# Seeding a PSUM bank, staging high parts in PSUM, longer runs for down weights and earlier raw loads in an attention, expert and feed-forward kernel

## The chip, the cores and the metric

The kernel runs on one core of a Trainium2 chip: TensorE multiplies matrices into PSUM, VectorE, ScalarE and GpSimd work elementwise, SyncE (SP) issues the transfers. GpSimd works on SBUF alone; VectorE and ScalarE read and write PSUM too. The metric is the device time of one execution in microseconds. Three runs took 2031.32 to 2033.63 us, median 2032.89.

## The reference

```python
scores = q @ k.T / sqrt(64)                       # 4 batches, 8 heads, 576 positions
mask: heads 0-3: 0 <= i - j < 32;  heads 4-7: i >= j and i % 32 == j % 32
x = (softmax(where(mask, scores, -1e9)) @ v)      # to 2304 tokens x 512
P = exp(x @ w_gate - max)                         # 2304 x 8
8 times: P /= P.sum(1) + 1e-9; P /= P.sum(0) + 1e-9; P *= 2304 / 8
x = sum over e of P[:, e] * (relu(x @ w1[e]) @ w2[e])         # 8 experts, 512 -> 1024 -> 512
h = x @ w_in                                                  # 512 -> 2048
out = (h * sigmoid(1.702 * h)) @ w_out                        # 2048 -> 512
```

All in float32. The kernel keeps that precision by splitting each operand into a high part (rounded to TensorE's fp32r) and a low part (the rest), and adds three products: high by high, high by low, low by high.

## The kernel before, in words

**Units.** The 2304 tokens are three blocks of 768. A unit is 256 hidden columns of one block: 32 units (8 experts by 4) for each block, then 8 for each block of the feed-forward layer, 120 in all. The first expert phase (block 0) is units 0 to 31, the second stage (blocks 1 and 2, where `seven(i)` holds) units 32 to 95, the ffn units 96 to 119.

**The up product** is not done as 8 block products but as 7 (`PRODUCTS`, line 44), with sums of input quarters (S1 to S4) and of weight quarters (T1 to T4). Each product is six matmuls of 384 columns (`sum_of_six`), and several add up in a PSUM bank: A takes X11, S2, S3 and X22; C takes S1 and S4; B takes X12. `product_and_after` (line 871) does what stands between the products: ScalarE copies a partial sum to SBUF (`copy_of`), VectorE adds it to a bank (`add`, line 868; line 887 for A plus a copy into B), and `activate` makes the hidden values: a high part on ScalarE (line 849), a low part on VectorE (line 852). X22 adds to bank A, so it waits until VectorE's addition of line 887 has read that bank.

**The down product** of units 0 to 31 and of the ffn is plain: six tiles a unit, six matmuls of 512 columns each (`tile_down`, lines 1080 to 1082), then VectorE adds the tile to the token sums (line 1099). In the second stage the down product is by sevens too (`chain`, line 976; VectorE adds at line 986).

**Weights.** In the first phase each unit's raw weights are loaded (`wa`, `wb`, 512 KB each), their quarters summed on GpSimd, and split by `split_into` (line 235): ScalarE rounds the high part (line 244), GpSimd or VectorE subtracts for the low part (line 238), a given number of pieces later, and SP stores both parts to DRAM, for the next phases (`s1moe`, `s7moe`). There VectorE makes the low parts of the up weights (w) and, for units whose first pass came too early, of recombined down weights (kw): `plan_down_sums` with `again` loads the raw down weights (raws) once more, subtracts (line 312) and splits.

**Order.** Nothing is reordered by a scheduler: the program is one list of pieces (13 a unit: 7 products and 6 down tiles), and `side[piece]` holds what is issued after that piece. Each engine takes its instructions in that order, and SP's transfers too. `piece_at(unit, k)` names a place in the list.

**PSUM** has eight banks. After the attention is done (`late`), they are A, A2, B, B2, C and three for down tiles (y, y, y3); `open_bank` alternates, and the gate's small products (`spare_bank`) borrow B or B2. While the attention still runs, A and B change places from unit to unit.

Of the kernel before, what the change touches and what calls it, by code (L numbers as in the profile page):

```python
# [47 lines left out]
    ("X12", "W21", "B", True, True),  # L48
# [8 lines left out]
def strided_attention_moe_ffn(  # L57
# [65 lines left out]
    late = []  # L123
    bank = {}
    turn_of = defaultdict(int)

    def open_bank(b, i):
# [107 lines left out]
    def split_into(t, src, kept, eng=nc.gpsimd, low=0, store=0):  # L235

        def rest():
            eng.tensor_tensor(out=t[:, 1, :], in0=src, in1=f(t[:, 0, :]), op=ALU.subtract)  # L238
# [5 lines left out]
        nc.scalar.activation(out=t[:, 0, :], in_=src, func=AF.Copy)  # L244
# [18 lines left out]
    def split_w1(i, k):  # L263
# [9 lines left out]
        if kind == "moe" and i > PLAIN:  # L273
            split_into(t, src, kept, nc.vector, *((5, 7) if PRODUCTS[k][0] == "X22" else (1, 3)))
        else:
            split_into(t, src, kept, store=2 if i > PLAIN else 0)

    def split_w2(i, ft):
        t = w2p.tile([P, 2, D], F32R, tag="w2", name="w2")
        _, kind, blk, n = UNITS[i]  # L280
        w2[i, ft] = t
        kept = sw2[n, ft].rearrange("p (h c) -> p h c", h=2) if kind == "ffn" else None
# [10 lines left out]
        split_into(t, raw[2, i][:, ft, :], kept, low=(0, 2 - ft)[i >= PLAIN], store=(0, 4)[i >= PLAIN])  # L293
# [5 lines left out]
    def plan_down_sums(dp, i, again=None):  # L299
# [14 lines left out]
        def split(k):  # L314
            t = dp.tile([P, 2, 2 * P], F32R, tag="kw", name="kw", bufs=5)
            src = down_sums[i][:, WHERE[PRODUCTS[k][1]][1], :]
            split_into(t, src, sw7[n, k].rearrange("p (h c) -> p h c", h=2), eng, 1 if again is None else 2, 3)
# [6 lines left out]
        if again is not None:  # L324

            side[piece_at(again, 0)].append(load)
# [3 lines left out]
        for m, k in enumerate(ks):  # L330
            at = piece_at(i, (6, 4)[i == S0 - 1] + m) if again is None else piece_at(again + 1, m)
# [45 lines left out]
    def plan_ahead(lo, hi):  # L377

        for n in range(AHEAD):
# [25 lines left out]
            def split_again(ft, r=r, n=n):  # L405
                t = r["kw"] if ft == 0 else r["sums"].rearrange("p q c -> p (q c)")
                t = t.rearrange("p (h c) -> p h c", h=2)
                src = r["raw"][:, ft * D : (ft + 1) * D]
                split_into(t.bitcast(F32R), src, sw2[n, ft].rearrange("p (h c) -> p h c", h=2), low=1, store=3)
# [69 lines left out]
    def input_sum(ph, m, eng):  # L479
        q = quarters(ph)  # L480
        what = PRODUCTS[m][0]
        if ph == 0:
            was = {"S3": "S1", "S4": "S2"}.get(what)
            xin[what, ph] = xin[was, ph] if was else rawp[0].tile([P, 2, NH], F32, tag=what, name=what)
        elif what == "S1":
# [5 lines left out]
            "S2": (xin.get(("S1", ph)), q["X11"], ALU.subtract),  # L491
# [921 lines left out]
```

## Time and profile before

| What | Before |
|---|---|
| median of 3 runs | 2032.89 us |
| profiled execution | 2031.87 us, span 2030.1 us, mean granted clock 0.993 |
| TensorE matmul busy | 1960.0 us (97%) |
| VectorE busy | 1610.9 us (79%) |
| GpSimd busy | 1233.5 us (61%) |
| ScalarE busy | 817.5 us (40%) |
| transfers | 548.32 MB, mean 270 GB/s |
| chain that ended last | PE 74%, DVE 13%, DMA 7%, POOL 2% |

The profile calls the engines PE (matmul), PEld (weight load), DVE (VectorE), ACT (ScalarE), POOL (GpSimd) and SP. TensorE's ends are modelled and its matmuls overlap, so its busy share is no measure of its pace; the number of matmuls in a stretch is.

How the views below are read. A row of busy time by stretch gives the stretch and its length in us, then the busy us and (x) the number of instructions of PE, PEld, DVE, ACT and POOL, then the granted clock, the mean share of the 16 DMA engines, and GB/s. A row of the waits gives the engine and line that waited, for whom, the us in total, how often, and the longest. A row of the timeline gives start, duration, engine, line, operation, and in brackets the idle time before it with what ended it. A row of the groups gives line, engine, operation, names (written <- read), shapes and count, then busy us, mean ns of one, and idle us before them with what ended it.

### The profile page before, as it was taken

How to read it: one execution, taken by the hardware profiler on the slowest of the kernel's cores; microseconds unless marked ns; L12 is line 12 of the kernel's file. 1: busy time of each engine (PE TensorE's matmuls, PEld its weight loads, DVE VectorE, ACT ScalarE, POOL GpSimd, SP SyncE). 2: the span in 40 equal slices, each digit the busy share in tenths (PEclk: the TensorE clock that was granted, in tenths of full speed). 3: DMA queues.
4: the chain of work that ended last, by engine and by line, in shares of the span. 5: the costliest groups of instructions: out<-in, count | busy, mean ns of one | idle time of the engine just before them, and what ended most of it. 6: DMA issues, size and time to landing. Idle time of an engine off the chain costs nothing.

```text
span 2030.1 us, 33823 instructions
## 1 busy us (share of the span) xinstructions
PE 1960.0 (97%) x10865; PEld 1800.8 (89%) x10865; DVE 1610.9 (79%) x2937; ACT 817.5 (40%) x2040; POOL 1233.5 (61%) x1201
## 2 busy tenths in 40 slices
PE   8999989898889999999999999999999999999999
PEld 6777778787778899999999999999999988898888
DVE  6777888897898788888788788999888666666666
ACT  6555534443445433333333433333333335533432
POOL 4443346686677777676767888878888747800200
PEclk9999999999999999999999999999999999999999
DMA  6356468999998798889888789998989957765663
GB/s 226 136 215 235 169 220 298 338 327 327 314 331 313 273 331 283 286 297 299 292 295 289 251 264 336 301 345 301 332 304 333 327 191 248 247 221 177 214 195 125
DMA packets 294640, 548.32 MB, mean 270 GB/s; under 512 B 30688, under 2 KB 75968, under 8 KB 293184
## 3 DMA queue, kind: packets, MB, share of 16 engines
q1 hardware_dynamic: 294176, 545.71, 78.3%
q8 instruction: 87, 1.43, 0.3%
q14 instruction: 89, 0.73, 0.1%
q10 hardware_dynamic: 288, 0.46, 0.1%
HBM read 384.52 MB, written 161.53 MB: 269 GB/s over the span
## 4 chain that ended last, share of the span: by engine, by line
PE 74%; DVE 13%; DMA 7%; POOL 2%; issue 2%; ACT 1%; SPq 1%; DVEq 0%; POOLq 0%; ACTq 0%
PE y L976 21%; PE pA L813 20%; PE pC L813 9%; PE y L1080 5%; PE y L1082 5%; PE y L1081 5%; PE pB L813 5%; DVE w L238 2%; DMA s1moe<-w 2%; DMA raws<-wb 2%; DMA s7moe<-kw 1%; DVE hl L852 1%; PE sc L589 1%; DVE acc L1099 1%; DVE kw L238 1%
## 5 line engine op out<-in xcount | busy, mean ns | idle before, releaser
L813 PE MATMUL pA<-xc,w 128*128 128x384 f32 x2880 | 583.1, 340 | 23.5 <-DVE pB L887 23.4
L813 PEld LDWEIGHTS pA<-xc,w 128*128 128x128 f32 x2880 | 510.5, 190 | 46.9 <-DVE pB L887 32.7
L976 PE MATMUL y<-comb,w 128*128 128x384 f32 x2688 | 538.9, 335 | 6.8 <-DVE sum L986 4.4
L976 PEld LDWEIGHTS y<-comb,w 128*128 128x128 f32 x2688 | 472.6, 188 | 9.0 <-DVE sum L986 6.1
L923 POOL TENSOR_TENSOR comb<-s,comb 128x384 fp32r<-128x384 f32 x256 | 280.9, 1109 | 71.0 <-ACT comb L918 65.7
L986 DVE TENSOR_TENSOR sum<-y,sum 128x384 f32<-128x384 f32 x420 | 230.4, 550 | 99.4 <-PE y L976 98.5
L813 PE MATMUL pC<-xc,w 128*128 128x384 f32 x1464 | 296.6, 337 | 0.0
L1080 PE MATMUL y<-w,hh 128*128 128x512 f32 x672 | 270.0, 402 | 10.2 <-ACT hh L849 9.6
L918 ACT ACTIVATE comb<-r 128x384 fp32r<-128x384 f32 x192 | 101.0, 526 | 432.1 <-DVE r L929 394.5
L1082 PE MATMUL y<-w,hl 128*128 128x512 f32 x672 | 269.7, 401 | 0.7 <-DVE hl L852 0.7
L813 PEld LDWEIGHTS pC<-xc,w 128*128 128x128 f32 x1464 | 257.9, 188 | 10.3 <-issue 0.7
L1081 PE MATMUL y<-w,hh 128*128 128x512 f32 x672 | 266.6, 397 | 0.0
L839 ACT ACTIVATE c<-pA 128x384 f32<-128x384 f32 x236 | 115.0, 487 | 145.3 <-PE pA L813 142.5
L238 POOL TENSOR_TENSOR w<-raw,w 128x512 fp32r<-128x512 f32 (+1 forms) x100 | 119.5, 1201 | 71.3 <-ACT w L244 62.7
L1080 PEld LDWEIGHTS y<-w,hh 128*128 128x128 f32 x672 | 127.6, 190 | 36.5 <-ACT hh L849 15.0
L1082 PEld LDWEIGHTS y<-w,hl 128*128 128x128 f32 x672 | 126.9, 189 | 34.0 <-DVE hl L852 5.5
L923 POOL TENSOR_TENSOR comb<-r,comb 128x384 fp32r<-128x384 f32 x64 | 68.0, 1063 | 145.1 <-ACT comb L918 144.2
L918 ACT ACTIVATE comb<-s 128x384 fp32r<-128x384 f32 x256 | 131.7, 514 | 28.8 <-POOL s L948 28.2
L813 PE MATMUL pB<-xc,w 128*128 128x384 f32 x708 | 142.7, 336 | 0.0
L1109 DVE TENSOR_TENSOR acc<-y,acc 128x512 f32<-128x512 f32 x126 | 86.5, 686 | 70.0 <-PE y L1082 69.4
L1081 PEld LDWEIGHTS y<-w,hh 128*128 128x128 f32 x672 | 127.5, 190 | 15.2
L948 POOL TENSOR_TENSOR s<-r,r 128x384 f32<-128x384 f32 x126 | 138.0, 1115 | 0.0
(154 smaller groups left out, 3015.7 us busy)
## 6 DMA issues: line engine op xcount, KB each, us to landing
w<-s1moe SPq DMA_DIRECT2D x448, 256.0 KB, 4.9
w<-s7moe SPq DMA_DIRECT2D x448, 256.0 KB, 4.9
s1moe<-w SPq DMA_DIRECT2D x216, 256.0 KB, 4.4
w<-s1ffn SPq DMA_DIRECT2D x133, 256.0 KB, 2.7
s7moe<-kw SPq DMA_DIRECT2D x128, 256.0 KB, 4.5
s7moe<-w SPq DMA_DIRECT2D x96, 256.0 KB, 4.4
w<-s2ffn SPq DMA_DIRECT2D x38, 512.0 KB, 4.0
raw<-wa SPq DMA_DIRECT2D x32, 512.0 KB, 6.7
```

Source lines behind the costliest of these rows:

```text
L238: eng.tensor_tensor(out=t[:, 1, :], in0=src, in1=f(t[:, 0, :]), op=ALU.subtract)
L813: nc.tensor.matmul(out=o, lhsT=w[:, hw, kk * P : (kk + 1) * P], rhs=x[:, hx, kk, :], start=opens and m == 0, stop=ends and m == len(todo) - 1,
L839: nc.scalar.activation(out=t, in_=bank[b][:, :NH], func=AF.Copy)
L918: nc.scalar.activation(out=t[:, 0, :], in_=part[i, q], func=AF.Copy)
L923: eng.tensor_tensor(out=t[:, 1, :], in0=part[i, q], in1=f(t[:, 0, :]), op=ALU.subtract)
L948: g.tensor_tensor(out=part[i, q], in0=part[i, a], in1=part[i, b], op=op)
L976: nc.tensor.matmul(out=o, lhsT=t[:, hw, dt * P : (dt + 1) * P], rhs=x[:, hx, :], start=(n == 0), stop=(n == 5))
L986: nc.vector.tensor_tensor(out=a, in0=o, in1=a, op=ALU.add)
L1080: nc.tensor.matmul(out=y, lhsT=hh[:, c], rhs=w[:, 0], start=(m == 0), stop=False)
L1081: nc.tensor.matmul(out=y, lhsT=hh[:, c], rhs=w[:, 1], start=False, stop=False)
L1082: nc.tensor.matmul(out=y, lhsT=hl[:, c], rhs=w[:, 0], start=False, stop=(m == 1))
L1109: nc.vector.tensor_tensor(out=a, in0=y, in1=a, op=ALU.add)
```

## The change

The copy of X11's sum goes into bank B, which X12 then adds to. The copy of A after S2 is added to C at once, and S4 adds on top. Bank B2 becomes a bank S with two halves, into which ScalarE writes the high part a second time wherever VectorE makes the low part; VectorE reads it there, and before a half is written again the subtraction that reads it is issued. Down weights lie as two column halves with their high and low parts side by side, so that a stored quarter is one run of 2 KB, and a down matmul reads its 512 columns as two runs of 256. The raw load of `again` is issued in the unit before, its splits are spread. Input sums on VectorE are done in halves, two of the four sums of unit 95 go to GpSimd, and there is one more piece between the gate's row and column steps.

```diff
-    ("X12", "W21", "B", True, True),
+    ("X12", "W21", "B", False, True),
...
         if late:
-            if b != "C" and turn_of[b] % 2:
-                pool, tag = late[0], b + "2"
-        elif i % 2:
+            if b == "A" and turn_of[b] % 2:
+                pool, tag = late[0], "A2"
+        elif i % 2 == 0:
             tag = {"A": "B", "B": "A", "C": "C"}[b]
... spare_bank
-        turn_of["B"] += 1
-        pool, tag = (late[0], "B2") if turn_of["B"] % 2 else (ps, "B")
-        return pool.tile(shape, F32, tag=tag, name=name)
+        turn_of["y"] += 1
+        if turn_of["y"] % 3 == 0:
+            return late[0].tile(shape, F32, tag="y3", name=name)
+        return ps.tile(shape, F32, tag="y", name=name, bufs=2)
... split_into
-        nc.scalar.activation(out=t[:, 0, :], in_=src, func=AF.Copy)
+        nc.scalar.activation(out=high, in_=src, func=AF.Copy)
+        if late and eng is nc.vector:
+            if not stage:
+                stage.append(late[0].tile([P, 2, 2 * P], F32R, tag="S", name="high"))
+            turn_of["S"] += 1
+            half = turn_of["S"] % 2
+            high = stage[0][:, half, :]
+            if half in staged:
+                staged[half]()
+            staged[half] = rest = once(rest)
+            nc.scalar.activation(out=high, in_=src, func=AF.Copy)
... split_w1
-            split_into(t, src, kept, nc.vector, *((5, 7) if PRODUCTS[k][0] == "X22" else (1, 3)))
+            split_into(t, src, kept, nc.vector, 1, 3)
... split_w2
-        t = w2p.tile([P, 2, D], F32R, tag="w2", name="w2")
+        t = w2p.tile([P, 2 * D], F32R, tag="w2", name="w2")
-                    c = (int(what[2]) - 1) * 2 * P
-                    kept.append((sw7[n, k].rearrange("p (h c) -> p h c", h=2), f(t)[:, :, c : c + 2 * P]))
+                    c = (int(what[2]) - 1) * D
+                    kept.append((sw7[n, k], f(t)[:, c : c + D]))
... plan_down_sums
-            side[piece_at(again, 0)].append(load)
+            side[piece_at(again - 1, 2)].append(load)
-            at = piece_at(i, (6, 4)[i == S0 - 1] + m) if again is None else piece_at(again + 1, m)
+            at = piece_at(i, (7, 4)[i == S0 - 1] + m) if again is None else piece_at(again + 1, 2 * m)
... plan_inputs
-            put(last - 1, 3, input_sum, ph, 4, v)
-            put(last - 1, 7, input_sum, ph, 5, v)
+            for h in range(2):
+                put(last - 1, 3 + h, input_sum, ph, 4, v, h)
+                put(last - 1, 6 + h, input_sum, ph, 5, v, h)
... gate_steps
-            steps += [sinkhorn_rows, lambda: None, lambda: None, sinkhorn_cols]
+            steps += [sinkhorn_rows, lambda: None, lambda: None, lambda: None, sinkhorn_cols]
... product_and_after
         if x == "X11":
-            snap["a"] = copy_of("A")
+            o = open_bank("B", i)[:, :NH]
+            nc.scalar.activation(out=o, in_=bank["A"][:, :NH], func=AF.Copy)
         elif x == "S2":
-            snap["u"] = copy_of("A")
+            add(copy_of("A"), "C", "C")
         elif x == "X12":
-            return go(i, "11", add(snap["a"], "B", "B"))
+            return go(i, "11", bank["B"][:, :NH])
         elif x == "S3":
-            if late:
-                o = open_bank("B", i)[:, :NH]
-                nc.vector.tensor_tensor(out=o, in0=bank["A"][:, :NH], in1=snap["c"], op=ALU.add)
-                return go(i, "22", o)
             return go(i, "22", add(snap["c"], "A", "B"))
         elif x == "S4":
-            return go(i, "12", add(snap["u"], "C", "C"))
+            return go(i, "12", bank["C"][:, :NH])
... down_input_sum, plan_seven
-        g = nc.vector if i == S1 - 1 else nc.gpsimd
+        eng = nc.vector if i == S1 - 1 and n % 2 else nc.gpsimd
-                put(u, 13, down_input_sum, u + 1, n)
+                put(u, 13 + (n // 2 if u + 1 == S1 - 1 else 0), down_input_sum, u + 1, n)
... tile_down
+            o = halves(y)
-            nc.tensor.matmul(out=y, lhsT=hh[:, c], rhs=w[:, 0], start=(m == 0), stop=False)
+            nc.tensor.matmul(out=o, lhsT=hh[:, c], rhs=w[:, 0], start=(m == 0), stop=False)
```

SP's queue in the first phase before, around the fifth repeated load of raw down weights (raws); kept are the 1.5 MB sums of the experts that waited for the gate:

```order
L213 DMA raw_5163<-wb 128x1024
L242 DMA s7moe<-w_5098 256x1x256 x2
L242 DMA s1moe<-w_5115 128x512
L242 DMA s7moe<-kw 128x512 x3
L1119 DMA acc<-kept 128x3072
L321 DMA raws_5207<-wb 128x1024
L206 DMA raw_5233<-wa 128x1024
```

The same place now:

```order
L214 DMA raw_5072<-wa 128x1024
L348 DMA raws_5078<-wb 128x1024
L252 DMA s1moe<-w_5039 128x512
L252 DMA s7moe<-kw 128x512
L252 DMA s1moe<-w_5055 128x512
L252 DMA s1moe<-w_5069 128x512
L252 DMA s7moe<-kw 128x512
L252 DMA s1moe<-w_5088 128x512
L252 DMA s7moe<-kw 128x512
L252 DMA s7moe<-w_5108 128x512
```

The load stands right behind the unit's first raw load, and the load of the kept sums (L1119 before, L1146 now) follows it after 16 further rows; the stores of down weights (s7moe<-w) are now 128 runs of 512 values in place of 256 of 256.

VectorE's queue in such a unit before, from X12 to the addition in front of X22:

```order
L312 TENSOR_TENSOR dsums<-raws_6417 128x256
L868 TENSOR_TENSOR pB<-pB,c 128x384
L312 TENSOR_TENSOR dsums<-raws_6417 128x256
L238 TENSOR_TENSOR w_6488<-sums,w_6488 128x256
L1099 SCALAR_TENSOR_TENSOR acc<-y,pr,acc 128x512
L852 SCALAR_TENSOR_TENSOR hl_6503<-pB,hh_6502 128x384
L312 TENSOR_TENSOR dsums<-raws_6417,dsums 128x256
L887 TENSOR_TENSOR pB<-pA,c 128x384
```

And now:

```order
L897 TENSOR_TENSOR pC<-pC,c 128x384
L248 TENSOR_TENSOR w_6546<-sums,high 128x256
L1126 SCALAR_TENSOR_TENSOR acc<-y,pr,acc 128x512
L339 TENSOR_TENSOR dsums<-raws_6329 128x256 x2
L248 TENSOR_TENSOR w_6579<-sums,high 128x256
L1126 SCALAR_TENSOR_TENSOR acc<-y,pr,acc 128x512
L881 SCALAR_TENSOR_TENSOR hl_6593<-pB,hh_6592 128x384
L339 TENSOR_TENSOR dsums<-raws_6329,dsums 128x256
L897 TENSOR_TENSOR pB<-pA,c 128x384
```

The addition to bank B after X12 is gone, the one to bank C stands ahead of X12's place, and each low part (w) reads the staged high part.

## Rows read from the trace of the kernel before

**Rows 1.** Busy time by stretch.

```profile
257.00:296.00 39.00, 35.58 (x171) 30.68 (x170) 33.71 (x79) 14.71 (x37) 16.11 (x18) 0.96 0.67 232
296.00:648.50 352.50, 317.25 (x1492) 272.30 (x1491) 317.76 (x517) 160.37 (x425) 239.74 (x253) 0.97 0.92 319
444.00:459.70 15.70, 15.70 (x80) 13.97 (x79) 15.11 (x26) 10.21 (x27) 13.24 (x15) 1.00 0.98 351
794.80:1100.60 305.80, 305.80 (x1766) 305.80 (x1766) 250.93 (x480) 99.62 (x211) 217.34 (x213) 1.00 0.87 288
1115.00:1619.00 504.00, 499.23 (x2859) 494.48 (x2858) 424.60 (x759) 176.79 (x378) 413.24 (x390) 1.00 0.89 310
1619.00:1663.70 44.70, 39.83 (x211) 38.06 (x210) 31.50 (x49) 15.64 (x29) 26.66 (x23) 0.96 0.63 205
1664.00:1800.00 136.00, 136.00 (x676) 121.17 (x675) 89.88 (x152) 66.36 (x147) 82.10 (x78) 1.00 0.69 241
1789.70:1867.90 78.20, 78.20 (x391) 70.29 (x390) 49.17 (x86) 26.58 (x55) 0.00 (x0) 1.00 0.57 186
```

**Rows 2.** Waits of TensorE from 296 to 648.5 us.

```profile
PE pA L813 <- DVE pB L887: 20.4, 15, 5.2
PE y L1080 <- ACT hh L849: 9.6, 10, 1.8
```

**Rows 3.** Timeline from 457 to 473 us: SP's queue, VectorE, TensorE.

```profile
458.15 0.59 SPq L321 DMA_DIRECT2D raws<-wb  x1
...
468.06 0.42 DVE L312 TENSOR_TENSOR dsums<-raws 128x256 f32<-128x256 f32 x1 [6.32 <-DMA raws<-wb]
...
472.31 0.69 PE L813 MATMUL pA<-xc,w 128*128 128x384 f32 x1 [5.18 <-DVE pB L887]
```

**Rows 4.** Groups of VectorE from 296 to 648.5 us.

```profile
L238 DVE TENSOR_TENSOR w<-sums,w 128x256 fp32r<-128x256 f32 x77 | 54.2, 704 | 0.0
L238 DVE TENSOR_TENSOR w<-raw,w 128x256 fp32r<-128x256 f32 x58 | 45.4, 795 | 0.0
L238 DVE TENSOR_TENSOR kw<-dsums,kw 128x256 fp32r<-128x256 f32 x36 | 36.8, 1022 | 0.0
...
L312 DVE TENSOR_TENSOR dsums<-raws 128x256 f32<-128x256 f32 x18 | 11.6, 647 | 21.8 <-DMA raws<-wb 21.8
...
L868 DVE TENSOR_TENSOR pB<-pB,c 128x384 f32<-128x384 f32 x19 | 10.5, 554 | 0.0
```

**Rows 5.** Groups of VectorE from 1900 to 2000 us, GpSimd idle.

```profile
L1109 DVE TENSOR_TENSOR acc<-y,acc 128x512 f32<-128x512 f32 x33 | 22.6, 686 | 20.0 <-PE y L1082 20.0
L862 DVE TENSOR_TENSOR hl<-sg,hh 128x384 fp32r<-128x384 f32 x26 | 14.5, 556 | 0.7
```

**Rows 6.** The same from 1664 to 1800 us, GpSimd busy.

```profile
L862 DVE TENSOR_TENSOR hl<-sg,hh 128x384 fp32r<-128x384 f32 x35 | 22.5, 643 | 0.7
```

**Rows 7.** A group of ScalarE from 296 to 648.5 us.

```profile
L244 ACT ACTIVATE w<-sums 128x256 fp32r<-128x256 f32 x77 | 31.5, 409 | 13.7 <-POOL sums L223 13.6
```

**Rows 8.** Waits of ScalarE from 296 to 648.5 us.

```profile
ACT hh L849 <- DVE pB L868: 99.9, 18, 9.3
...
ACT kw L244 <- DMA s7moe<-kw: 12.5, 11, 2.8
```

**Rows 9.** Transfers from 296 to 648.5 us; issues: count, KB each, us to landing.

```profile
DMA packets 59146, 112.38 MB, mean 319 GB/s; under 512 B 5751, under 2 KB 20439, under 8 KB 58605
...
s7moe<-w SPq DMA_DIRECT2D x57, 256.0 KB, 4.5
```

**Rows 10.** Busy time in the two stretches of 50 us with most bytes.

```profile
368.00:418.00 50.00, 47.77 (x228) 40.77 (x228) 47.06 (x71) 24.20 (x66) 35.11 (x36) 0.99 1.00 352
1438.00:1488.00 50.00, 49.24 (x283) 48.72 (x283) 41.95 (x82) 17.16 (x37) 41.20 (x39) 1.00 0.98 359
```

**Rows 11.** Waits of TensorE from 1619 to 1663.7 us.

```profile
PE y L976 <- DVE sum L986: 4.4, 2, 4.2
```

**Rows 12.** The gate's matmuls by line: ns min/median/max.

```profile
L731 PE MATMUL pl<-x,wgr x96: 326/326/350, 96.0 to 256.7; 128*32 128x192 f32 x96
```

More of the change, by code (lines that the diff above doesn't have):

```diff
@@ L123, in strided_attention_moe_ffn, with once @@
     late = []
+    stage = []
+    staged = {}
+    def once(fn):
+        todo = [fn]
+        return lambda: todo.pop()() if todo else None
     bank = {}
@@ L235, in split_into @@
     def split_into(t, src, kept, eng=nc.gpsimd, low=0, store=0):
+        high = t[:, 0]
         def rest():
-            eng.tensor_tensor(out=t[:, 1, :], in0=src, in1=f(t[:, 0, :]), op=ALU.subtract)
+            eng.tensor_tensor(out=t[:, 1], in0=src, in1=f(high), op=ALU.subtract)
         def keep():
@@ L273, in split_w1, with by_part, halves @@
         if kind == "moe" and i > PLAIN:
-            split_into(t, src, kept, nc.vector, *((5, 7) if PRODUCTS[k][0] == "X22" else (1, 3)))
+            split_into(t, src, kept, nc.vector, 1, 3)
         else:
             split_into(t, src, kept, store=2 if i > PLAIN else 0)
+    def by_part(t):
+        return t.rearrange("p (q h c) -> p h q c", q=2, h=2)
+    def halves(src):
+        return src.rearrange("p (q c) -> p q c", q=2)
     def split_w2(i, ft):
-        t = w2p.tile([P, 2, D], F32R, tag="w2", name="w2")
+        t = w2p.tile([P, 2 * D], F32R, tag="w2", name="w2")
         _, kind, blk, n = UNITS[i]
-        w2[i, ft] = t
-        kept = sw2[n, ft].rearrange("p (h c) -> p h c", h=2) if kind == "ffn" else None
+        w2[i, ft] = by_part(t)
+        kept = sw2[n, ft] if kind == "ffn" else None
         if not fresh(i):
@@ L290, in split_w2 @@
                 if what[0] == "W" and int(what[1]) == ft + 1:
-                    c = (int(what[2]) - 1) * 2 * P
-                    kept.append((sw7[n, k].rearrange("p (h c) -> p h c", h=2), f(t)[:, :, c : c + 2 * P]))
-        split_into(t, raw[2, i][:, ft, :], kept, low=(0, 2 - ft)[i >= PLAIN], store=(0, 4)[i >= PLAIN])
+                    c = (int(what[2]) - 1) * D
+                    kept.append((sw7[n, k], f(t)[:, c : c + D]))
+        split_into(by_part(t), halves(raw[2, i][:, ft, :]), kept, low=(0, 2 - ft)[i >= PLAIN], store=(0, 4)[i >= PLAIN])
     down_sums = {}
@@ L406, in split_again @@
                 t = r["kw"] if ft == 0 else r["sums"].rearrange("p q c -> p (q c)")
-                t = t.rearrange("p (h c) -> p h c", h=2)
                 src = r["raw"][:, ft * D : (ft + 1) * D]
-                split_into(t.bitcast(F32R), src, sw2[n, ft].rearrange("p (h c) -> p h c", h=2), low=1, store=3)
+                split_into(by_part(t.bitcast(F32R)), halves(src), [(sw2[n, ft], t)], low=1, store=3)
             tasks = [open_and_load, lambda: None, lambda: None, sums] + [lambda m=m, r=r: r["todo"][m]() for m in range(4)]
@@ L477, in quarters, with input_sum @@
         return {"X11": x[:, 0:2, 0:NH], "X12": x[:, 2:4, 0:NH], "X21": x[:, 0:2, NH:BT], "X22": x[:, 2:4, NH:BT]}
-    def input_sum(ph, m, eng):
+    def input_sum(ph, m, eng, h=slice(0, 2)):
         q = quarters(ph)
         what = PRODUCTS[m][0]
-        if ph == 0:
+        if (what, ph) in xin:
+            pass
+        elif ph == 0:
             was = {"S3": "S1", "S4": "S2"}.get(what)
@@ L490, in input_sum @@
             "S1": (q["X21"], q["X22"], ALU.add),
-            "S2": (xin.get(("S1", ph)), q["X11"], ALU.subtract),
+            "S2": (xin["S1", ph], q["X11"], ALU.subtract),
             "S3": (q["X11"], q["X21"], ALU.subtract),
@@ L494, in input_sum @@
         }[what]
-        eng.tensor_tensor(out=xin[what, ph], in0=a, in1=b, op=op)
+        eng.tensor_tensor(out=xin[what, ph][:, h], in0=a[:, h], in1=b[:, h], op=op)
     def input_of(ph, m):
@@ L946, in down_input_sum @@
         part[i, q] = hp.tile([P, NH], F32, tag="hl" + slot, name="s" + slot, bufs=2 if slot == "22" else 1)
-        g = nc.vector if i == S1 - 1 else nc.gpsimd
-        g.tensor_tensor(out=part[i, q], in0=part[i, a], in1=part[i, b], op=op)
+        eng = nc.vector if i == S1 - 1 and n % 2 else nc.gpsimd
+        eng.tensor_tensor(out=part[i, q], in0=part[i, a], in1=part[i, b], op=op)
     def sum_input(i, q):
@@ L1079, in tile_down @@
             w = w2[i, m]
-            nc.tensor.matmul(out=y, lhsT=hh[:, c], rhs=w[:, 0], start=(m == 0), stop=False)
-            nc.tensor.matmul(out=y, lhsT=hh[:, c], rhs=w[:, 1], start=False, stop=False)
-            nc.tensor.matmul(out=y, lhsT=hl[:, c], rhs=w[:, 0], start=False, stop=(m == 1))
+            o = halves(y)
+            nc.tensor.matmul(out=o, lhsT=hh[:, c], rhs=w[:, 0], start=(m == 0), stop=False)
+            nc.tensor.matmul(out=o, lhsT=hh[:, c], rhs=w[:, 1], start=False, stop=False)
+            nc.tensor.matmul(out=o, lhsT=hl[:, c], rhs=w[:, 0], start=False, stop=(m == 1))
         tt = blk * TB + t
```

4 lines of the change are left out of this document (2 added, 2 removed).

## The prediction

> **What bounds the kernel now.** I read the busy time by stage first, to see where TensorE is not at its pace. Two stretches of the trace give that pace: the five ffn units from 1789.7 to 1867.9 us take 78.2 us, 15.64 us a unit of 78 matmuls, and the 21 units of the second stage from 794.8 to 1100.6 take 305.8 us, 14.56 us a unit of 84 [rows 1]. There the clock is full and nothing of the other engines shows. The time is lost elsewhere. The stretch from 296.0 to 648.5 us is 19 units of the first expert phase (10 to 28, each counted from its X12 product): at 15.64 us they would need 297 us and they take 352.5, so 55 us are lost in this one stage. 257 to 296 loses about 6 (two units, 31.3 us, and the gate's small matmuls), 1115 to 1619 loses 8 (2,859 matmuls at 84 in 14.56 us need 495.6), and 1619 to 1663.7, where the second stage turns into the third, loses 8 of the same count (211 matmuls, 36.6 us).
>
> In the 19 units I looked next at TensorE's waits: 20.4 us for the addition of line 887, which must read bank A before X22 may add to it, and 9.6 us for a high part of hidden values, which hangs on another VectorE addition [rows 2]. The granted clock is 0.97 over the stretch, so some 21 us of it ran at half clock and cost 10 more [rows 1]. All of it follows VectorE, which is busy 317.8 of 352.5 us and so has no room to catch up. The timeline of one stall shows what puts it behind [rows 3]: the late load of a raw down weight is issued at 458.15 (the order of SP's queue has it right behind a 1.5 MB load of kept sums), VectorE stands 6.32 us at its first subtraction, and TensorE then stands 5.18 us in front of X22. VectorE waits for such loads 21.8 us in all, 8 times [rows 4].
>
> **The change, part by part.** Against the profiled execution, 2031.87 us with a span of 2030.1; the median of the runs shown is 2032.89, 1.0 us above it.
>
> *Low parts from the PSUM bank.* VectorE makes 77 + 58 + 36 low parts of 256 columns in the stage, at 704, 795 and 1022 ns [rows 4]; all read two SBUF tiles. How long one takes undisturbed: a 384-column subtraction of two SBUF tiles takes 556 ns where GpSimd is idle [rows 5] and 643 where it is 60% busy [rows 6], while VectorE's additions with one PSUM operand take 554 in the middle of the stage with GpSimd 68% busy [rows 1, 4]. So the excess is contention with GpSimd and a PSUM operand is free of it. An addition of 512 columns takes 686 [rows 5], so a column costs (686 - 554) / 128 = 1.03 ns, and 256 columns 554 - 132 = 422 ns; the subtraction that ends the stall in the timeline, of this size, took 0.42 as well [rows 3]. That saves 77 x 0.28 + 58 x 0.37 + 36 x 0.60 = 65 us of VectorE. The bounds: nothing, if the first operand alone still collides, and 65.
>
> [...]
>
> ScalarE pays: 171 further copies of 256 columns. It never writes PSUM from SBUF before; the nearest row, SBUF to SBUF, is 409 ns [rows 7], so 70 us more on 160.4, 73% of a stage of 320. I cost that at nothing for TensorE, since ScalarE is idle more than half of the stage now and is itself kept waiting by VectorE's additions (99.9 us for one of them) [rows 8]; the cover is gone if ScalarE has to wait for VectorE at each of these copies (the third rival).
>
> *One addition less.* The copy of X11's sum goes into bank B and X12 adds on top, so one of the two additions of line 868 goes: 19 x 0.554 = 10.5 us of VectorE here, 0.55 us a unit everywhere. The copy was there before, of the same columns. X12 now waits for it, but it is released two products and three down pieces earlier, so nothing is late. The addition for S4 moves three products ahead, off the way from S4 to its activation; bank C is added to again only five pieces later.
>
> *Raw loads sooner.* The load now goes out 11 places of the piece list earlier, on the same queue, and ahead of the kept sums instead of behind them. From issue to the first subtraction it took 9.9 us; 11 pieces more are over 13 us. The 21.8 us of waiting go. What the load is moved past on SP's queue are the stores of one unit; it has to wait for its single buffer, which VectorE left half a unit earlier.
>
> *VectorE after.* 317.8 - 65 - 10.5 = 242 us busy for 19 units, 12.7 us a unit, under TensorE's 15.64. So VectorE is no longer the bound, and without the gain of the low parts it would have 307 us of work, near 320 with its waits for TensorE.
>
> *What is late next.* The stage moves 112.38 MB [rows 9]. The best 50 us of the stage ran at 352 GB/s with the DMA engines' share at 1.00, and the best of the whole trace at 359 with 0.98 [rows 10]. 112.38 MB at 352 GB/s are 319 us. The 57 stores of down weights that went out in 1 KB runs [rows 9] become 2 KB runs: 14,592 packets become half as many. What a packet saves the rows don't show; the byte rates bound it: the stretch at 359 GB/s has nearly all 2 KB packets and is 2% faster over all bytes, and these stores are 13% of the bytes. Nothing to 6 us; I take 2. Queue gaps cost 3 back (the stage's share now is 0.92, the best 50 us have 1.00): 320 us, **32 us gained**, between 0 and 54 (TensorE's pace).
>
> [...]
>
> *Gate and two down-bank turns.* In 257 to 296 and at the start of the next stage TensorE waits for the gate's column sums; one more piece between rows and columns, with a quicker VectorE, takes 3.5 of the 6 us. The gate now borrows a down bank instead of B; a late reader there would cost one down piece (1.4 us at most: 15.64 less 42 up matmuls at 14.56 / 84, by six) some 16 times, but only if VectorE is behind.
>
> *Second stage.* VectorE 84% busy loses 0.55 us of work a unit; I take 3 of the 8 us, since the input sums in halves also let the addition before X22 through. Bounds 0 and 6.
>
> *Turn at 1638.* TensorE waits 4.4 us for sums there [rows 11], behind four subtractions and additions in a row on VectorE. Two go to GpSimd, but the last then waits for GpSimd's, and GpSimd has its own queue of low parts, 26.66 us in these 44.7 [rows 1]. I take 1.5 us gained, between 6 gained and 2 lost.
>
> *Attention overlap.* 6 additions less, 1.5 us, between 0 and 4.
>
> *Down products over two runs.* 2,016 matmuls read 512 columns as two runs of 256. The nearest row is far: the gate's matmuls read 192 columns as six runs of 32, and all 96 take 326 to 350 ns, most of them 326 [rows 12]. I take zero. If all of that spread of 24 ns came from the five steps between runs, a step would cost 5 ns and the 2,016 matmuls 10 us. A gain is excluded, since the same columns pass.
>
> Sum: 32 + 3.5 + 3 + 1.5 + 1.5 = 41.5 us. 2031.9 - 41.5 = 1990, 1991 beside the median; I say **1990**.
>
> **The rivals.** *TensorE's pace is reached.* If the DMA engines take more than 352 GB/s, or loads and stores shift into the emptier units behind, the stage falls to 297 and some 4 us: 51 gained, 61 with the rest: 1972 beside the median. For it: the unit at 444 us took 15.70 us in the middle of this stage [rows 1]. Against: the share of 1.00 in its best 50 us, and that only every second unit has the late load's extra traffic.
>
> *A fuller queue.* The stage stays at the transfers' present efficiency, 319 GB/s at a share of 0.92 raised to 335 at 0.97, since buffers (five for the recombined weights) wait for their stores more often when the units are shorter: 335 us, 17 gained, 26 with the rest: 2007. For it: ScalarE already waits for such stores, 11 times [rows 8], and DMA shares of 0.92 over a whole stage leave little. Against: the early loads take away a burst.
>
> *ScalarE is tied to VectorE (slower).* Two half banks mean that each staged copy waits until VectorE has read the one two before it; behind it in ScalarE's queue stand the activations that TensorE waits for. ScalarE would have 160 + 70 = 230 us of work, so it takes 352.5 us and more when the wait is over 0.7 us for each of the 171. At 0.9 us the stage is 384 us, 31 lost, some 5 of the other gains left: 2059. For it: VectorE was up to 6 us late. Against: its load falls to three quarters.
>
> *The change does not do what it says:* if the PSUM operand doesn't shorten the low parts, VectorE has 307 us and the stage still shrinks to about 325, the loads alone being worth 22: 27 gained and 8 with the rest, 1998, inside the forecast's own range.
>
> **How the numbers follow.** Forecast, 1978 to 2000: 0.52. TensorE's pace, 1964 to 1978: 0.22. A fuller queue, 2000 to 2018: 0.18. Slower: 0.05. No change: 0.03. The range from 1968 to 2016 leaves out a fifth of the second case below (0.04), and above an eighth of the third (0.02) and the last two (0.08), in all under 2 in 10. 0.2%, 4 us, is about what a measurement of this kernel can tell from no change: faster 0.92, within 0.03, slower 0.05.
>
> **What would show it.** In the changed profile: VectorE's low parts near 0.42 us and equal among themselves; no wait of VectorE for raw down weights; VectorE's busy share in the stage near 75% and the DMA share near 0.98 with about 350 GB/s; TensorE's waits in the stage now ending at ScalarE or DMA, not at the addition in front of X22; a granted clock near 1.00 there. I am wrong in the step on the transfers if the stage takes 300 us, and in the step on ScalarE's cover if its staged copies wait long for VectorE. Down matmuls spaced wider in the ffn units than 15.64 us a unit allows would show the cost of the two runs.

## The result and the profile after

The changed kernel takes 1981.78 us (median of 4 runs, 1979.59 to 1983.04), beside 2033.26 for the kernel before on the same chip: a ratio of 0.9744, 95% interval 0.9727 to 0.9761, 51.5 us faster. The profiled execution took 1983.04 us with a span of 1981.3. The forecast was 1990, range 1968 to 2016.

Each stretch below runs from a unit's X12 product to another's, so that the kernels can be compared row by row:

| Units | Before, us | After, us | Gained | Forecast |
|---|---|---|---|---|
| start to 2 | 118.3 | 119.3 | -1.0 | 0 |
| 2 to 8, attention overlap | 138.6 | 138.7 | -0.1 | 1.5 |
| 8 to 10, gate | 39.0 | 35.9 | 3.1 | 3.5 |
| 10 to 29, the stage | 352.6 | 317.9 | 34.7 | 32 |
| 29 to 61 | 466.6 | 464.6 | 2.0 | 0 |
| 61 to 95, second stage | 503.8 | 499.4 | 4.4 | 3 |
| 95 to 97, turn | 44.8 | 39.8 | 5.0 | 1.5 |
| 97 to the end | 366.4 | 365.7 | 0.7 | 0 |

The busy time by stretch after, columns as in [rows 1]: gate, stage, the unit at 444 us, 50 us of the stage, second stage, turn, five ffn units.

```profile
258.00:293.90 35.90, 33.77 (x170) 29.04 (x167) 27.56 (x70) 17.03 (x46) 18.25 (x21) 1.00 0.76 261
293.90:611.80 317.90, 306.04 (x1494) 270.83 (x1493) 248.25 (x506) 219.56 (x605) 221.71 (x252) 0.98 0.98 354
444.00:459.70 15.70, 15.70 (x80) 14.12 (x79) 10.75 (x21) 7.68 (x21) 10.71 (x13) 1.00 1.03 397
341.00:391.00 50.00, 46.89 (x224) 41.20 (x223) 36.94 (x71) 31.12 (x84) 33.11 (x39) 0.97 1.03 389
1076.40:1575.80 499.40, 496.39 (x2858) 494.83 (x2858) 406.52 (x731) 177.56 (x378) 409.07 (x389) 1.00 0.90 312
1575.80:1615.60 39.80, 38.33 (x212) 36.58 (x212) 29.36 (x46) 15.67 (x29) 28.14 (x25) 1.00 0.69 237
1741.90:1820.10 78.20, 78.20 (x392) 70.29 (x391) 46.97 (x82) 27.17 (x55) 0.00 (x0) 1.00 0.59 185
```

In the stage VectorE fell from 317.8 to 248 us and ScalarE rose from 160 to 220 [rows 1]. The same bytes now pass at 354 GB/s with a share of 0.98. The ffn units still take 15.64 us each.

VectorE's and ScalarE's groups in the stage after (293.9 to 611.8 us):

```profile
L248 DVE TENSOR_TENSOR w<-sums,high 128x256 fp32r<-128x256 f32 x77 | 31.8, 413 | 19.0 <-issue 12.9 <-ACT high L264 5.7
L248 DVE TENSOR_TENSOR w<-raw,high 128x256 fp32r<-128x256 f32 x59 | 24.4, 414 | 17.0 <-ACT high L264 17.0
L248 DVE TENSOR_TENSOR kw<-dsums,high 128x256 fp32r<-128x256 f32 x36 | 14.9, 414 | 7.8 <-ACT high L264 4.2 <-issue 2.0 <-POOL dsums L339 1.0
L339 DVE TENSOR_TENSOR dsums<-raws 128x256 f32<-128x256 f32 x18 | 14.3, 835 | 0.0
L897 DVE TENSOR_TENSOR pB<-pA,c 128x384 f32<-128x384 f32 x19 | 10.5, 554 | 0.0
...
L254 ACT ACTIVATE w<-sums 128x256 fp32r<-128x256 f32 x77 | 31.2, 406 | 0.0
L264 ACT ACTIVATE high<-sums 128x256 fp32r<-128x256 f32 x77 | 29.7, 386 | 21.0 <-DVE w L248 20.1
```

The low parts took 704, 795 and 1022 ns [rows 4]; with the PSUM operand all three take 413 or 414, though GpSimd is 70% busy beside them. The subtraction that still reads two SBUF tiles (dsums) did not get quicker: 835 ns against 647. The loads of raws cost VectorE no wait any more. A copy into the bank takes ScalarE 386 ns, less than the 406 of the one into SBUF.

Waits in the same stretch after (who waited for whom, us in total, times, longest):

```profile
ACT high L264 <- DVE w L248: 33.2, 67, 2.6
ACT kw L254 <- DMA s7moe<-kw: 10.1, 9, 3.0
PE y L1107 <- ACT hh L878: 4.1, 2, 3.1
PE pA L842 <- ACT c L868: 3.2, 1, 3.2
PE pA L842 <- DVE pB L897: 1.3, 2, 0.7
POOL sums L231 <- DVE w L248: 1.0, 1, 1.0
```

TensorE's 20.4 us of waiting for the addition before X22 have become 1.3 [rows 2]. The largest of what is left are two stalls, of 3.09 and 3.25 us. The timeline of the first, ScalarE and TensorE from 371 to 375 us (columns as in [rows 3]), and then the row of busy time behind it:

```profile
371.32 0.42 ACT L254 ACTIVATE kw<-dsums 128x256 fp32r<-128x256 f32 x1 [2.97 <-DMA s7moe<-kw]
...
374.05 0.50 PE L1107 MATMUL y<-w,hh 128*128 128x512 f32 x1 [3.09 <-ACT hh L878]
```

```profile
374.00:381.00 7.00, 6.96 (x26) 5.87 (x27) 4.43 (x9) 4.87 (x14) 6.19 (x8) 0.76 1.05 382
```

ScalarE stands 2.97 us for a kw buffer whose store is under way, the activation behind it is late, TensorE stands 3.09 us, and then works on at a clock of 0.76: this unit takes 21.0 us instead of 15.64, so 3.1 us of waiting and the lower clock behind it cost 5.4 together.

### The profile page after: what moved, and what is told of

It reads as the page before. It is cut to its first block, busy times and chain, and to the rows that moved or that the text cites. A ratio compares the mean times of both kernels' runs of the same rounds, so it can differ in the third digit from the quotient of the medians.

```text
span 1981.3 us, 33759 instructions
## 1 busy us (share of the span) xinstructions
PE 1941.6 (98%) x10865; PEld 1798.3 (91%) x10865; DVE 1488.4 (75%) x2827; ACT 883.7 (45%) x2241; POOL 1211.8 (61%) x1203
## 4 chain that ended last, share of the span: by engine, by line
PE 66%; DVE 2%; POOL 1%; DMA 1%; issue 0%; ACT 0%; ACTq 0%
PE y L1002 22%; PE pA L842 18%; PE pC L842 9%; PE pB L842 5%; PE y L1109 4%; PE y L1108 4%; PE y L1107 4%; DMA w<-s1moe 0%; DVE xs L523 0%; POOL s L974 0%; POOL comb L949 0%; DMA w<-s7moe 0%; DVE comb L949 0%; POOL xc L538 0%; DVE xc L542 0%
## 5 line engine op out<-in xcount | busy, mean ns | idle before, releaser
L842 PE MATMUL pA<-xc,w 128*128 128x384 f32 x2880 | 574.9, 336 | 6.9 <-DVE pB L897 3.7
L842 PEld LDWEIGHTS pB<-xc,w 128*128 128x128 f32 x708 | 125.1, 188 | 5.0 <-issue 0.3
```

Of the source, the lines that this page charges most:

```text
L842: nc.tensor.matmul(out=o, lhsT=w[:, hw, kk * P : (kk + 1) * P], rhs=x[:, hx, kk, :], start=opens and m == 0, stop=ends and m == len(todo) - 1,
```

## The experiments

Changed kernel means the kernel after; its stage is 317.9 us. Shown are the lines as in the experiment (+) against the kernel it starts from (-); three dots stand for further lines. The times of a stage come from one profiled execution a run. How far they scatter shows the run called noturn below, whose edit is at unit 95 alone:

```profile
294.60:610.30 315.70, 304.78 (x1495) 270.07 (x1494) 246.50 (x502) 218.91 (x603) 221.76 (x252) 0.99 0.98 356
```

Its stage takes 2.2 us less than the changed kernel's, so smaller differences of the stage are not told from nothing.

**Without the staged high parts** (nostage), from the changed kernel:

```diff
-        if late and eng is nc.vector:
+        if False:
```

> The changed kernel without the staging bank: VectorE's low parts read two SBUF tiles again, ScalarE's second copies go. Theory A (VectorE's work set the pace of the first phase): its low parts return to 0.7 to 1.0 us, its busy time in the 19 units rises from 248 to some 310 us, TensorE waits for it again, and the kernel takes 1990 to 1998 us, 8 to 16 more than the changed one (1981.8). Rival B (the early raw loads alone mattered, VectorE had room): within 3 us of 1981.8, since the work still fits into 318 us.

Measured: 1990.59 us (0.9785 of before, 0.9771 to 0.9800), 8.8 us over the changed kernel; stage 325.4. VectorE's groups there and ScalarE's wait:

```profile
L248 DVE TENSOR_TENSOR w<-sums,w 128x256 fp32r<-128x256 f32 x77 | 53.4, 693 | 3.9 <-issue 3.9
L248 DVE TENSOR_TENSOR w<-raw,w 128x256 fp32r<-128x256 f32 x58 | 44.9, 788 | 0.0
```

```profile
ACT kw L254 <- DMA s7moe<-kw: 35.4, 16, 4.8
```

The low parts are slow again, so the PSUM operand is what made them quick; but 53 us of VectorE's busy time (301.7 against 248.3) are worth 7.5 us of the stage. What grows with them is ScalarE's wait for a kw buffer whose store is under way, from 10.1 to 35.4 us; that TensorE loses its time by this way is read from the rows and not shown (oldruns below has 17.7 us of this wait at no cost).

**Raw loads at their old place** (lateload), from the changed kernel:

```diff
-            side[piece_at(again - 1, 2)].append(load)
+            side[piece_at(again, 0)].append(load)
```

> The changed kernel with the repeated raw load at its old place. Theory A: VectorE waits for the loads again, some 20 us in all, but now has 70 us of room in the stage, so TensorE feels only the longest: 1988 to 1994 us, 6 to 12 more. Rival B (the loads were the whole gain of the stage): 20 to 28 more, 2002 to 2010.

Measured: 1981.44 us (0.9742, 0.9728 to 0.9757), stage 318.8. VectorE's and TensorE's waits in it, and the row of the stage:

```profile
DVE dsums L339 <- DMA raws<-wb: 23.0, 8, 4.8
...
PE pA L842 <- DVE pB L897: 7.7, 8, 2.0
...
PE pA L842 <- ACT c L868: 1.7, 2, 1.3
PE y L1107 <- ACT hh L878: 0.9, 1, 0.9
```

```profile
291.80:610.60 318.80, 303.97 (x1495) 266.49 (x1494) 241.83 (x505) 218.10 (x605) 220.60 (x252) 1.00 0.97 354
```

All 23.0 us of the wait are back and cost 0.9 us of the stage, nothing of the time. My expectation of a loss was wrong. VectorE's 70 us of slack do not take all of it up: TensorE's wait for the addition before X22 rises from 1.3 to 7.7 us. But its waits for ScalarE fall from 7.3 us to 2.6, the two long stalls are gone, and the granted clock is 1.00 instead of 0.98. Why they go, no run shows.

**Raw loads alone** (b_load), the same edit in the kernel before:

```diff
-            side[piece_at(again, 0)].append(load)
+            side[piece_at(again - 1, 2)].append(load)
```

> The kernel before with the repeated raw loads 11 pieces sooner and nothing else. Theory A (VectorE had no room): its 21.8 us of waiting go, the 19 units fall from 352.5 to some 330 us, the kernel takes 2009 to 2016 us. Rival D (the waits were covered even then, as they are in the changed kernel with late loads): within 5 us of 2034.

Measured: 2023.92 us (0.9954, 0.9939 to 0.9969), stage 343.3.

```profile
ACT kw L244 <- DMA s7moe<-kw: 29.8, 22, 5.7
PE y L1080 <- ACT hh L849: 19.1, 11, 5.4
PE pA L813 <- DVE pB L887: 4.3, 7, 1.1
```

TensorE's wait at X22 falls from 20.4 to 4.3 us, but its wait for the hidden values' high part doubles from 9.6 [rows 2] as ScalarE's wait for kw buffers goes from 12.5 [rows 8] to 29.8. Of 21.8 us, 9.3 arrive: less than theory A asks for, more than rival D.

**The seed alone** (b_seed): in the kernel before, X11's copy into bank B, S2's sum into C, and the banks that go with it.

```diff
-    ("X12", "W21", "B", True, True),
+    ("X12", "W21", "B", False, True),
...
+            o = open_bank("B", i)[:, :NH]
+            nc.scalar.activation(out=o, in_=bank["A"][:, :NH], func=AF.Copy)
...
+            add(copy_of("A"), "C", "C")
```

> The kernel before with the banks and additions of the change alone (X11 into B, the early addition to C, the gate in the down banks), no staging, late loads. Theory A: 10.5 us of VectorE's work less in the 19 units and 0.55 us a unit elsewhere, 2018 to 2023 us. Rival E (what counts is that nothing stands between S4 or X12 and its activation, not VectorE's work): the waits for hidden values go too, 2005 to 2015.

Measured: 2022.81 us (0.9952, 0.9934 to 0.9971), stage 347.2; the second stage (units 61 to 95):

```profile
1110.10:1607.50 497.40, 496.16 (x2858) 494.86 (x2857) 404.49 (x726) 177.14 (x378) 408.61 (x389) 1.00 0.91 314
```

503.8 before, 497.4 with the seed, 20 us less work for VectorE: the seed's edits, taken together, account for all of the second stage's gain (4.4 in the changed kernel). In the first-phase stage they give 5.4 us; the waits there:

```profile
PE pA L814 <- DVE pB L869: 20.8, 15, 2.7
...
ACT kw L245 <- DMA s7moe<-kw: 36.7, 19, 7.6
```

In units 2 to 8, the attention overlap, they cost 2.9 us:

```profile
117.20:258.70 141.50, 131.04 (x887) 101.88 (x884) 104.75 (x227) 70.81 (x251) 53.40 (x51) 1.00 0.59 207
```

**Seed and staged high parts** (b_seed_stage), the seed's edits and besides, in `split_into`:

```diff
+        if late and eng is nc.vector:
...
+            staged[half] = rest = once(rest)
+            nc.scalar.activation(out=high, in_=src, func=AF.Copy)
```

> The same and the staging bank, still with late loads and 1 KB runs. Theory A: VectorE's busy time in the 19 units falls to 245 us, its waits for loads are covered, the 19 units take 318 to 324 us, the kernel 1988 to 1996. Rival B (the loads mattered): above 2005.

Measured: 2005.62 us (0.9868, 0.9847 to 0.9889), stage 334.8, not the 318 to 324 that I expected:

```profile
295.60:630.40 334.80, 311.95 (x1492) 273.23 (x1491) 249.01 (x496) 219.74 (x602) 220.43 (x254) 0.97 0.96 337
```

VectorE had 249.0 us of work as in the changed kernel, so VectorE's load wasn't what lacked. GpSimd's waits, first in the kernel before and then in this one:

```profile
POOL sums L223 <- DVE w L238: 67.9, 19, 5.5
```

```profile
POOL sums L231 <- DVE w L248: 46.2, 17, 4.2
```

GpSimd can't write the next sums of weight quarters while VectorE still has to read the tile, and that was the low part of X22's weight, five pieces late. In the changed kernel it is 1.0. The two next experiments price this edit and the other one on times of splits.

**X22's low part late again** (lowx22), from the changed kernel:

```diff
-            split_into(t, src, kept, nc.vector, 1, 3)
+            split_into(t, src, kept, nc.vector, *((5, 7) if PRODUCTS[k][0] == "X22" else (1, 3)))
```

> The changed kernel, in which only the low part of X22's up weight is again made five pieces after its high part instead of one. Theory M (GpSimd's sums of weight quarters wait for the tile that this late low part still reads: 67.9 us of such waits in the kernel before, 46.2 with the seed and the staging alone, 1.0 in the changed kernel; this edit is most of what those two edits alone lacked): GpSimd's wait for VectorE is back at 30 to 50 us, the stage of 19 units takes 328 to 332 us instead of 317.9, the time is 1991 to 1996. Theory T (in the changed kernel the transfers set the stage, as they did when the kept loads were split, and an engine off the path may wait): GpSimd's wait is back too, but the stage stays within 315 to 321 us and the time within 4 us of 1982.

Measured: 1991.31 us (0.9806, 0.9785 to 0.9827). The stage and the wait:

```profile
298.90:625.30 326.40, 308.02 (x1495) 272.32 (x1494) 249.47 (x505) 220.59 (x605) 223.93 (x254) 0.98 0.95 344
```

```profile
POOL sums L231 <- DVE w L248: 34.3, 18, 3.5
ACT kw L254 <- DMA s7moe<-kw: 20.8, 12, 4.7
```

8.5 us of stage and 9.5 of time for one pair of numbers, as much as the staged high parts at the end. The edit reaches back to the weights of unit 3, and the attention overlap, units 2 to 8, loses too, 5.6 us against the changed kernel:

```profile
118.70:263.00 144.30, 133.86 (x889) 104.08 (x885) 104.88 (x227) 71.11 (x252) 53.41 (x51) 0.98 0.58 203
```

The profiled execution was the slowest of the four (1989.57 to 1996.45 us) and both losses together exceed the 9.5 of the median, so in the median run the stage's part may be less than 8.5.

**Recombined down weights split at the old places** (kwplace), from the changed kernel:

```diff
-            split_into(t, src, sw7[n, k].rearrange("p (h c) -> p h c", h=2), eng, 1, 3)
+            split_into(t, src, sw7[n, k].rearrange("p (h c) -> p h c", h=2), eng, 1 if again is None else 2, 3)
-            at = piece_at(i, (7, 4)[i == S0 - 1] + m) if again is None else piece_at(again + 1, 2 * m)
+            at = piece_at(i, (6, 4)[i == S0 - 1] + m) if again is None else piece_at(again + 1, m)
```

> The changed kernel, in which the recombined down weights are split at the places of before: one piece apart instead of two, and with the low part two pieces after the high part instead of one. Theory M (the spread of these splits is a part of what the seed and the staging alone lacked, because ScalarE then makes a high part, a staged copy and the activations in the same pieces): the stage takes 321 to 326 us, the time is 1985 to 1990, with more half clock. Theory T (transfers set the stage): the stage stays within 315 to 321 us, the time within 4 us of 1982.

Measured: 1985.89 us (0.9773, 0.9751 to 0.9795), stage 323.8:

```profile
ACT kw L254 <- DMA s7moe<-kw: 16.3, 14, 4.0
PE pA L842 <- ACT c L868: 8.5, 5, 3.7
```

5.9 us of the stage. With a unit's four splits in consecutive pieces ScalarE waits more for kw buffers (10.1 before this edit), and its copies out of the banks, for which TensorE waits, come late more often (3.2). The first of these waits alone is not the price: oldruns below has 17.7 us of it at no cost.

**Old runs for the expert down weights** (oldruns), from the changed kernel:

```diff
-        w2[i, ft] = by_part(t)
+        old = kind == "moe"
+        flat = t.rearrange("p (h c) -> p h c", h=2)
+        w2[i, ft] = flat if old else by_part(t)
...
-                    kept.append((sw7[n, k], f(t)[:, c : c + D]))
+                    kept.append((sw7[n, k].rearrange("p (h c) -> p h c", h=2), f(flat)[:, :, c : c + 2 * P]))
...
-            o = halves(y)
+            o = y if kind == "moe" else halves(y)
```

> The changed kernel with the expert phase's down weights in their old layout: stored in 1 KB runs, down matmuls of that phase reading 512 columns in one run. If transfers bind the 19 units all through (share 0.98), the 14,592 packets of 1 KB cost 3 to 4 us more than the 7,296 of 2 KB, and the kernel takes 1985 to 1986. Rival C (only a few bursts and the buffers behind them bind): within 1 us of 1981.8. If two runs cost a matmul something, it is faster than the changed kernel.

Measured: 1982.91 us (0.9748, 0.9734 to 0.9763), stage 316.6. ScalarE's wait in it:

```profile
ACT kw L254 <- DMA s7moe<-kw: 17.7, 11, 4.8
```

The 1 KB runs cost nothing that can be measured, and the two-run matmuls neither (the ffn units, 15.64 us before and after, show these by themselves). The expected 3 to 4 us, for transfers that bind all through, did not come.

**Kept sums in six loads each, a unit earlier** (keptsplit), from the changed kernel:

```diff
-            nc.sync.dma_start(out=back[e].rearrange("p t d -> p (t d)"), in_=kept[e])
+            nc.sync.dma_start(out=back[e][:, t, :], in_=kept[e, :, t * D : (t + 1) * D])
...
-            side[piece_at(u, 0)].append(lambda e=e: load(e))
...
+                side[piece_at(u - 1, 2 * t)].append(lambda e=e, t=t: load(e, t))
```

> The changed kernel with each 1.5 MB load of kept sums cut into six of 256 KB, issued over the unit before its first use. Theory F (what is left in the stage are bursts: ScalarE waits for the buffers of recombined weights behind that load, in the units at 360 and 460 us): the two stalls and their half-clock stretches go, 7 to 12 us less, 1970 to 1975. Rival G (the transfers bind all through at a share of 0.98): the bytes are the same, within 2 us of 1981.8.

Measured: 1981.28 us (0.9743, 0.9726 to 0.9761), stage 318.7. The stall at 374 is gone and one of 3.3 us stands a unit earlier:

```profile
DVE acc L1124 <- DMA kept<-acc: 9.5, 1, 9.5
PE y L1107 <- DVE acc L1124: 3.3, 1, 3.3
```

VectorE needs the accumulator whose 1.5 MB store is now under way beside the loads. The stall moves, the time stays. As the earlier loads bring a wait of their own, this run does not tell transfers from buffers.

**The same, with kw stored a piece sooner** (kept_store2), meant to beat both:

```diff
-            split_into(t, src, sw7[n, k].rearrange("p (h c) -> p h c", h=2), eng, 1, 3)
+            split_into(t, src, sw7[n, k].rearrange("p (h c) -> p h c", h=2), eng, 1, 2)
```

> A version meant to beat both: the changed kernel with the 1.5 MB load of the kept sums in three loads of 0.5 MB two pieces apart, started one unit earlier, and the recombined down weights stored one piece sooner, so that ScalarE waits less for a free buffer (10.1 us in the changed kernel). If buffers held by stores still cost TensorE its two stalls of 3 us and the half clock behind them, the stage falls from 317.9 to 308 to 312 us and the time to 1972 to 1977. If the transfers set the stage at their share of 0.98, the stalls move and the stage stays within 315 to 321 us, the time within 4 us of 1982.

Measured: 1983.31 us (0.9764, 0.9748 to 0.9780), stage 318.3. Its loads are the same six of 256 KB, not the three that the expectation names. Nothing gained; no version beat the changed kernel.

**The turn's sums all on VectorE** (noturn), from the changed kernel:

```diff
-        eng = nc.vector if i == S1 - 1 and n % 2 else nc.gpsimd
+        eng = nc.vector if i == S1 - 1 else nc.gpsimd
-                put(u, 13 + (n // 2 if u + 1 == S1 - 1 else 0), down_input_sum, u + 1, n)
+                put(u, 13, down_input_sum, u + 1, n)
```

> The changed kernel with all four input sums of unit 95 on VectorE in one place again. Theory: the stall of 4 us at the turn to the ffn units comes back with a stretch at half clock, 1985 to 1987 us, 4 to 5 more. Rival (the turn gained from VectorE's smaller load before it): within 1 us of 1981.8.

Measured: 1986.19 us (0.9762, 0.9745 to 0.9778), 4.4 over the changed kernel. The turn and TensorE's wait in it:

```profile
1574.40:1618.40 44.00, 39.53 (x212) 38.09 (x212) 31.80 (x48) 15.69 (x29) 26.51 (x23) 0.96 0.66 214
```

```profile
PE y L1002 <- DVE sum L1012: 4.0, 1, 4.0
```

Against 39.8 us and a clock of 1.00 in the changed kernel: of the 4.2 us between them the wait, as in [rows 11], is 4.0 where the changed kernel has 1.0. The two sums on GpSimd, with two of the four one piece later, remove it; the run does not tell the two edits apart.

**The gate with two empty pieces** (oldgate), from the changed kernel:

```diff
-            steps += [sinkhorn_rows, lambda: None, lambda: None, lambda: None, sinkhorn_cols]
+            steps += [sinkhorn_rows, lambda: None, lambda: None, sinkhorn_cols]
```

> The changed kernel with the gate's steps as before, two empty pieces between rows and columns instead of three. The prediction gave 3.5 us to this part. Theory G (the piece is worth that, at TensorE's waits for the column sums): from the X12 of unit 8 to that of unit 12 the changed kernel took 71.1 us, this one takes 74 to 77, the time is 1985 to 1988. Rival (VectorE, with its shorter work, was what made the gate late, and the piece is worth nothing by itself): within 1 us of 71.1, and the time within 4 us of 1982.

Measured: 1983.81 us (0.9762, 0.9745 to 0.9779).

```profile
257.50:329.10 71.60, 67.26 (x338) 58.28 (x335) 60.29 (x156) 38.18 (x104) 40.58 (x47) 1.00 0.74 253
```

From unit 8 to 12 that is 71.6 us against 71.1. As noturn, which has the piece, takes 71.5, nothing is left that the piece is worth by itself. Before, these four units took 78.8; without the staged high parts they take 75.4, with X22's low part late 73.1. So the gate's gain hangs on edits that gave VectorE and GpSimd room, not on the piece.

## Why the prediction was right, and where it was not

The sign, the stage and the state at the end came as forecast: the stage at 318 us with 354 GB/s at a share of 0.98 (forecast 320, about 350, 0.98), low parts at 414 ns (422), 65 us of VectorE's work less by them (65), ScalarE near 220 (230). The granted clock in the stage is 0.98, where near 1.00 was forecast. Profile against profile the forecast is 7.3 us short (48.8 gained, 41.5 forecast): the turn 3.5, the stage 2.7, small gains behind it 2.7 (2.0 to unit 61, 0.7 from 97), the second stage 1.4, less 1.6 of the attention overlap, 1.0 of the start and 0.4 of the gate.

**The stage's 32 us were right in size, its steps were not.** The step that failed is the account of VectorE: it let the low parts, the addition and the raw loads carry the stage to the transfers' limit, and gave the two edits on times of splits no price. Added one after the other to the kernel before, seed and staging bring it to 334.8, VectorE already relieved of 69 us; the other 17 us came with the rest. Taken out of the changed kernel one at a time, the stage loses

| Taken out | us of the stage |
|---|---|
| X22's low part one piece after its high part | 8.5 |
| staged high parts | 7.5 |
| splits of recombined weights two pieces apart | 5.9 |
| raw loads sooner | 0.9 |
| one more gate piece | 0.5 |
| 2 KB runs | -1.3 |

The last three are not told from nothing (noturn's 2.2). The first three sum to 21.9, not 34.7. The seed was not taken out of the changed kernel (alone it gave 5.4), and the parts cover for one another: raw loads are worth 9.3 alone and 0.9 last. How the 12.8 us between are shared by the two is not shown. What I had not read is GpSimd's 67.9 us of waiting for VectorE in the kernel before. I counted VectorE's busy time and not who waits for its late instruction. How the wait reaches TensorE (GpSimd's own low parts late, then their stores, then ScalarE's buffer) is read from the rows, and only the price of the edit is shown.

**Raw loads.** "The 21.8 us of waiting go" was right; that they are worth 22 us by themselves, as the rival of a change that does not do what it says had it, was not: b_load gave 9.3.

**The transfers' limit.** The 320 us rested on 352 GB/s as the best 50 us. The changed kernel moved 389 over 50 us, so the 352 were what the kernel before asked for, not what the engines can do. The kernel before had itself gone past 352 for shorter times: its transfers from 300 to 600 us, in 40 slices of 7.5 us each, reach 394.

```profile
GB/s 213 382 141 202 380 303 375 360 259 370 382 290 348 357 329 368 321 291 309 382 304 381 367 330 292 251 341 346 289 349 253 335 342 243 360 394 334 350 289 370
```

So it was luck that the stage came out at 318 beside the 320 that the 352 gave: at 389 GB/s its 112.5 MB would take 289 us (an estimate from that row), under TensorE's 297. What holds the stage there stays open. For transfers speak 354 GB/s at a share of 0.98 over all of it, and that keptsplit, kept_store2 and lateload end within 318.3 to 318.9 us, each with other stalls. Against them speak oldruns, where 7,296 packets more cost nothing, and the single units. Eleven of the 19 take 15.64 us, TensorE's pace; this is one of them (its ends rounded to 0.1 us):

```profile
344.80:360.40 15.60, 15.60 (x80) 14.02 (x78) 11.25 (x22) 9.30 (x27) 11.25 (x14) 1.00 1.05 402
```

The 20.7 us over that pace lie in units 10, 11, 14, 17, 20 and 24 to 26. No run took bytes away; and lowx22 and kwplace show that a bad order still holds the stage above 318.

**Fewer packets** were given 2 us and gave none that can be measured (oldruns). **Down products over two runs** cost nothing, as taken.

**The gate**: 3.5 forecast, 3.1 measured, for a wrong reason (oldgate). **Second stage**: 3 forecast, 4.4 measured, and the seed's edits are its cause (b_seed, 6.4 without the halved input sums that the forecast counted on). **Attention overlap**: 1.5 forecast, none. With the seed and X22's low part still late these units take 141.5 us (b_seed, b_seed_stage), with the low part sooner 138.7 (lowx22, where it is late again, 144.3), against 138.6 before: the seed's edits cost some 3 us and the earlier low part gave them back; the forecast had neither. **Turn**: 1.5 forecast, 5.0 measured: I feared GpSimd's queue, which had room, and left out what the row of the stretch had at hand, the clock of 0.96 [rows 1] behind a wait of 4.4 us. In the changed kernel, with a wait of 1.0 us there, the clock is 1.00 (noturn, with 4.0, has 0.96).

**The rivals.** TensorE's pace (297 us) was not reached: the two units with a stall and a granted clock of 0.50 behind it (5.4 and 6.0 us over 15.64) and units 10, 11 and 24 to 26 make the difference. The fuller queue is what b_load, b_seed and nostage looked like, with ScalarE waiting 30 to 37 us for kw buffers and stages of 325 to 347 us. With the staged high parts that wait is 8 to 21 us in every run (11.0 in b_seed_stage, which has late splits), but its size does not decide: b_seed_stage takes 334.8 us. ScalarE does wait for VectorE at 67 of its staged copies, 33.2 us in all: 0.2 us a copy over 171, well under the 0.7 from which that rival decides.

## What to carry to other kernels

Busy time of the late engine is half an account: look also at who waits for its late instruction, and price every edit that only moves an instruction, since here one pair of numbers was worth as much as the new PSUM bank. A wait removed alone returned part of its length, and another wait took its place (b_load gave 9.3 of 21.8 us, and ScalarE's wait for buffers held by stores rose from 12.5 to 29.8); in the changed kernel the same wait came back at no cost, while other waits shrank (lateload). The best rate of a stretch is a floor of what the transfer engines can do, not their limit: the best 50 us of the stage ran at 352 GB/s before, and 50 us of the changed kernel at 389.

## What the runs showed of the hardware

The subtraction of 256 columns that makes a low part takes 413 or 414 ns with one operand in PSUM and 651 to 1022 with both in SBUF (means of the groups before and in nostage), GpSimd at some 70% beside it. ScalarE wrote 256 columns of the sums into PSUM in 386 ns and into SBUF in 406. Stores in 1 KB and in 2 KB runs gave the same time within what can be measured (stages of 316.6 us in oldruns and 317.9 in the changed kernel). Beside both long stalls of TensorE in the changed kernel the granted clock stood at 0.50 for a part of the time (from 376 to 379 us and from 465 to 471; 0.76 on average over the 7 us behind the first, 0.84 over the unit of the second): with stalls of 3.09 and 3.25 us these units took 5.4 and 6.0 us more than 15.64. In the kernel before it stood at 0.50 from 472 to 478 us, at the end of the stall of [rows 3] and behind it: the half clock of the prediction is this level. One core moved 389 GB/s over 50 us (341 to 391 us of the changed kernel), loads and stores together.
